# First MoE weight column of batch 0 multiplied inside the last attention units

## The chip, the core and the metric

The kernel runs on one NeuronCore of a Trainium2 chip. The core has five engines with queues of their own: PE (TensorE, matmuls), DVE (VectorE), ACT (ScalarE), POOL (GpSimd, which also issues DMAs here) and SP (SyncE, which here only issues DMAs). Each queue runs its instructions strictly in the order in which they were written, and semaphores hold an instruction until what it reads, or the buffer it overwrites, is ready. The metric is the time of one execution on the device in microseconds (us); lower is better.

## The reference, cut to what matters

```
scores = scale * q @ k.T ; mix the 12 heads by w_pre
attn   = exp(scores - max) / (sum + 1e-9) ; mix the 12 heads by w_post
x      = attn @ v, written as tokens x (12 heads * 64) = 1792 x 768
out    = ((x @ w_a) * (x @ w_b)) @ w_out          # 768 -> 1536 -> 768
```

There are 4 batches of 448 tokens. The second half is called MoE below, after the names in the code.

## The kernel before, in words

**Attention.** The queries of a batch are cut into units of 20 tokens, 23 units per batch, 92 in all, numbered 0 to 91. One loop (lines 695 to 729) writes the program: in its step s it writes unit s's parts for all engines. On PE these are the head mixing `mp` (L308), one score product for a later chunk of queries (`pst`, L244; up to step 82 only), one slice of attn @ v (`xp`, L387) and the second head mixing `pp` (L351) of unit s-1. DVE takes the row maximum `nm` (L318), a copy of the score product in two units of three, and, once ACT has summed the exponentials, three small operations (L331 to L334). ACT computes the exponentials (L321) and copies `pp` out of PSUM (L366). POOL issues the DMAs (L288) that gather unit s+4's scores into `sb`. SP loads q, k and v, stores x to DRAM (`xd`), and once per unit writes one number of `nm` (`paced`, L202), which keeps its queue at the pace of the units. The last steps, 92 and 93, and the code behind the loop finish the last slices of `xp`.

**MoE.** Every product is made of three fp32r matmuls of 448 columns per 128-row block: high half of the weights times both halves of x, and low half of the weights times the high half of x. A column is 128 of the 1536 hidden features. For one column and one batch, `run_a` (into `pa`) and `run_b` (into `pb`) take 18 matmuls each (6 blocks of 3); ACT copies `pa` to `sa`, DVE multiplies `pb` by it into `hf`. So that weights and x are ready in halves, two preparations exist:

- The weights come as 64-bit floats. `to_f32` makes 32-bit floats of one side (w_a or w_b) of a column with six DVE operations and one POOL addition (L502 to L508), then ACT and POOL split them into `wh` and `wl` (L538, L539). `r` (`cvr`) has one buffer, `m` (`cvm`) three.
- x of batch b is loaded from `xd` by six DMAs (`load_x`, L465), and split per block by one ACT copy (L471) and one DVE subtraction (L472).

`order` is the list of the conversions: entry 0 is w_a of column 0, entry 1 is w_b of column 0, entry 2 is w_a of column 1. `plan_moe` puts the first of this work into the attention loop by tables: `todo_at[s]` runs at the start of step s, `at_end[s]` at its end. `s0` is 83. Before the change the weights of entries 0 and 1 are loaded in three DMAs of 256 KB each in units 74 to 76 and 78 to 80; the conversion of entry 0 stands at the ends of steps 78 to 83, that of entry 1 at 84 to 89, and x(0) is loaded in steps 81 to 86 and split in steps 90 to 92. All MoE matmuls stand behind the loop, from `run_a(0, 0)` on.

`plan_loads` distributes q, k and v loads over the steps: each has a first and a last step, and takes the one with the fewest bytes planned so far.

Of the kernel before, what the change touches and what calls it, by code (L numbers as in the profile page):

```python
# [21 lines left out]
def talking_heads_bilinear_kernel(  # L22
# [11 lines left out]
    nc = tc.nc  # L34
# [86 lines left out]
    def ps_t():  # L121
        return ps.tile([128, 2, 512], F32, tag="t", name="pst", bufs=1)[:, 0]
# [3 lines left out]
    def later(fn, n=3):  # L126
        todo_at.setdefault(now[0] + n, []).append(fn)
# [295 lines left out]
    def plan_loads():  # L423
        per_b, row = NC // B, 4 * 128
        wants, busy = [], [0] * (NU + 8)
        for (a, p), u in av_at.items():
            if p % 3 == 2 and u < NU:
                busy[u + 1] += row * 3 * QU * groups[a][2]
        for u in range(V_FIRST, V_FIRST + V_PIECES // 2):
            busy[u] += row * S  # L430
        for c in range(3, NC):
            b, t0, n = chunks[c]
            for j in range(G // QG):
                last = qk_at[c, QG * j] - LEAD
                wants.append((max(last, 0), max(last - 2, 0), row * QG * n, (load_q, c, j)))
            for i in range(G if t0 == 0 else 0):
                n = G * b + i - 10
                first = qk_at[per_b * (n // G) + per_b - 1, n % G] + 1 if n >= 0 else 0
                wants.append((qk_at[c, i] - LEAD, first, row * S, (load_k, b, i)))
        for b in range(1, B):  # L440
            first = max(av_at[per_b * (b - 2) + per_b - 1, H // 2 - 1] + 1 if b > 1 else 0, V_FIRST + V_PIECES // 2)
            for i in range(V_PIECES):
                wants.append((av_at[per_b * b, i // 2] - V_LEAD, first, row * S // 2, (load_v, b, i)))
        for last, first, n, it in sorted(wants, key=lambda w: w[0]):
            u = min(range(min(first, last), last + 1), key=lambda u: (busy[u], -u))
            busy[u] += n
            after.setdefault(u, []).insert(0, it)
# [46 lines left out]
    def to_f32(u):  # L494
        t = raws.pop(u)
        lo, hi = t[:, :, 0], t[:, :, 1]
        m = mc.tile([128, CW], I32, tag="m", name="cvm", bufs=3)
        r = mc.tile([128, CW], I32, tag="r", name="cvr", bufs=1)
        mf = m.bitcast(F32)
        ts, stt = nc.vector.tensor_scalar, nc.vector.scalar_tensor_tensor  # L500
        return m.rearrange("p (k f) -> p k f", k=KD), [
            lambda: ts(m, hi, 0x7FFFFFFF, None, op0=ALU.bitwise_and),  # L502
            lambda: ts(r, lo, 28, 1, op0=ALU.logical_shift_right, op1=ALU.bitwise_and),
            lambda: ts(mf, mf, F64_TOP, 2.0**-112, op0=ALU.min, op1=ALU.mult),
            lambda: ts(m, m, 3, None, op0=ALU.logical_shift_left),
            lambda: stt(m, hi, -(1 << 31), m, op0=ALU.bitwise_and, op1=ALU.bitwise_or),
            lambda: stt(m, lo, 29, m, op0=ALU.logical_shift_right, op1=ALU.bitwise_or),  # L507
            lambda: nc.gpsimd.tensor_tensor(m, m, r, op=ALU.add),  # L508
        ]

    def conv_f(u):
        kind, f, e = u
# [42 lines left out]
    def run_a(f, b):  # L555
        hh, ll = wt["f", f]
        x = xt[b]
        pa = ps.tile([128, 512], F32, tag="m", name="pa", bufs=3)[:, :S]
        mm3(pa, hh, ll, x[:, 0], x[:, 1], KD)
# [4 lines left out]
    def run_b(f, b):  # L564
        hh, ll = wt["f", f]
        x = xt[b]
        pb = (ps_t() if f == b == 0 else ps.tile([128, 512], F32, tag=f"p{b % 2}", name="pb", bufs=1))[:, :S]
        mm3(pb, hh, ll, x[:, 0], x[:, 1], KD, KD)
# [49 lines left out]
    def plan_moe():  # L618
        o, fin = {}, {}

        def at(n, *fns):
            at_end.setdefault(n, []).extend(fns)

        def load(n, fns):
            for i, fn in enumerate(fns):
                todo_at.setdefault(n + i, []).append(fn)

        def op(u, j):
            def run():
# [8 lines left out]
        todo_at.setdefault(RAW_AT[0], []).append(lambda: load(RAW_AT[0] + 1, load_raw(order[0], 3)))
        todo_at.setdefault(RAW_AT[1], []).append(lambda: load(RAW_AT[1] + 1, load_raw(order[1], 3)))
        s0 = last_prep + 1  # L640
        for j in range(KD):
            at(s0 - 5 + j, op(0, j))
            at(s0 + 1 + j, op(1, j))
            todo_at.setdefault(s0 - 2 + j, []).append(lambda j=j: load_x(0, (j,)))
# [12 lines left out]
    with tc.manual_schedule():
# [37 lines left out]
        for s in range(NU + 2):  # L695
            now[0] = s
            if s == last_prep + 1:
                open_moe()
            while nxt_g <= min(s + AH, NU - 1) and ready.get(units[nxt_g][0], -1) < s:
                gather(nxt_g)  # L700
                nxt_g += 1
            if 0 <= s - V_FIRST < V_PIECES // 2:
                for p in range(2):
                    load_v(0, 2 * (s - V_FIRST) + p)
            for fn in todo_at.pop(s, ()):
                fn()
            if s < NU:
                premix(s)
            if 2 <= s <= NU:
                evac_p(s - 2)  # L710
            if s < NU:
                for k_ in blocks_of(s):
                    smax(k_)
            for it in items.get(s, ()):
                if it[0] is qk:
                    it += (it[2] % OWN if s not in late else 1,)
                it[0](*it[1:])
            if s < NU:
                norm(s)
            if 0 <= s - 1 < NU:  # L720
                postmix(s - 1)
            for it in late.get(s, ()):
                qk(*it[1:], 0)
            for it in after.get(s, ()):
                it[0](*it[1:])
            for fn in at_end.pop(s, ()):
                fn()
            if s == NU:
                evac_p(NU - 1)
        for p in range(6):  # L730
            av(NA - 1, p)
        for t in sorted(todo_at):
# [130 lines left out]
```

## Time and profile before

| | us |
|---|---|
| three runs | 899.97, 918.04, 918.10 |
| median of the runs | 918.04 |
| the profiled execution, its own time | 903.93 |
| its span, first to last instruction | 902.2 |
| PE busy in the span | 868.3 (96%) |
| DVE busy | 518.8 (57%) |
| POOL busy | 442.5 (49%) |
| ACT busy | 377.5 (42%) |

The profile is of one execution. PE's matmuls overlap one another, so PE can be counted as busy and still not run at its densest: a matmul of 448 columns is counted with 0.36 us, while the next one starts 0.20 us later. A bracket at the end of a row of the timeline gives the idle time of the engine ahead of that row and what ended it; "issue" there means that the engine waited for nothing that the profile shows. Times in the rows are from the start of the span.

### The profile page before, as it was taken

How to read it: one execution, taken by the hardware profiler on the slowest of the kernel's cores; microseconds unless marked ns; L12 is line 12 of the kernel's file. 1: busy time of each engine (PE TensorE's matmuls, PEld its weight loads, DVE VectorE, ACT ScalarE, POOL GpSimd, SP SyncE). 2: the span in 40 equal slices, each digit the busy share in tenths (PEclk: the TensorE clock that was granted, in tenths of full speed). 3: DMA queues.
4: the chain of work that ended last, by engine and by line, in shares of the span. 5: the costliest groups of instructions: out<-in, count | busy, mean ns of one | idle time of the engine just before them, and what ended most of it. 6: DMA issues, size and time to landing. Idle time of an engine off the chain costs nothing.

```text
span 902.2 us, 27078 instructions
## 1 busy us (share of the span) xinstructions
PE 868.3 (96%) x11440; PEld 703.2 (78%) x11440; DVE 518.8 (57%) x907; ACT 377.5 (42%) x848; POOL 442.5 (49%) x547
## 2 busy tenths in 40 slices
PE   8888999999999897899999999999999999999998
PEld 3455666565666554699999999999999989999997
DVE  5666777677777675577656665557554545151500
ACT  5666777667677665531111111111111244343531
POOL 4586777677766754124333432233232245455552
PEclk9999999999999999999999999999999999999999
DMA  6797676767666965734533433334332664646441
GB/s 161 175 212 182 177 196 191 172 181 188 181 162 180 213 179 126 228 135 136 171 118 124 153 124 136 118 119 136 118 126 87 240 245 149 258 136 258 140 147 61
DMA packets 81850, 147.45 MB, mean 163 GB/s; under 512 B 41758, under 2 KB 61322, under 8 KB 80706
## 3 DMA queue, kind: packets, MB, share of 16 engines
q1 hardware_dynamic: 53602, 108.05, 37.4%
q0 software_dynamic: 28128, 37.68, 16.5%
q8 instruction: 90, 1.47, 0.7%
q14 instruction: 30, 0.25, 0.1%
HBM read 80.23 MB, written 26.74 MB: 119 GB/s over the span
## 4 chain that ended last, share of the span: by engine, by line
PE 76%; POOL 8%; issue 6%; DMA 5%; DVE 2%; ACT 1%; SPq 1%; POOLq 0%; ACTq 0%; DVEq 0%
POOL sb L288 6%; PE pa L549 6%; PE pa L550 6%; PE pa L551 6%; PE po L550 6%; PE po L551 6%; PE po L549 6%; PE pb L550 6%; PE pb L549 6%; PE pb L551 6%; PE xp L387 6%; PE pp L351 5%; PE mp L308 4%; PE pst L244 4%; DMA sb<-s 2%
## 5 line engine op out<-in xcount | busy, mean ns | idle before, releaser
L288 POOL DMA_DIRECT2D sb<-s x350 | 202.6, 589 | 91.1 <-PE mp L308 49.3
L508 POOL TENSOR_TENSOR cvm<-cvm,cvr 128x768 int32<-128x768 int32 x36 | 66.4, 1844 | 196.9 <-DVE cvm L507 196.9
L318 DVE TENSOR_REDUCE nm<-mp 124x1 f32<-124x448 f32 x180 | 104.6, 619 | 67.5 <-PE mp L308 66.4
L539 POOL TENSOR_TENSOR wl<-v,wh 128x768 fp32r<-128x768 f32 x48 | 93.4, 1965 | 100.7 <-ACT wh L538 100.7
L321 ACT ACTIVATE a<-mp,nm 124x448 f32<-124x448 f32 x180 | 112.8, 631 | 57.5 <-DVE nm L318 57.4
L387 PEld LDWEIGHTS xp<-pt,v 120*64 120x64 f32 x1536 | 76.5, 140 | 67.2 <-issue 45.2
L561 ACT COPY sa<-pa 128x448 f32<-128x448 f32 x48 | 25.8, 537 | 227.6 <-PE pa L551 227.6
L351 PE MATMUL pp<-kr,a 60*56 60x60 f32 x5760 | 104.6, 216 | 13.4 <-issue 12.8
L351 PEld LDWEIGHTS pp<-kr,a 60*56 60x56 f32 x5760 | 90.1, 127 | 31.4 <-issue 20.6
L366 ACT COPY pt<-pp 120x480 f32<-120x480 f32 x176 | 91.2, 574 | 50.8 <-PE pp L351 50.7
L308 PE MATMUL mp<-sb,wp 60*64 60x448 f32 x720 | 100.9, 545 | 6.4 <-ACT a L321 3.0
L571 DVE TENSOR_TENSOR hf<-pb,sa 128x448 f32<-128x448 f32 x47 | 29.4, 625 | 132.6 <-PE pb L551 118.8
L550 PE MATMUL po<-hl,wh 128*128 128x448 f32 x288 | 104.5, 363 | 0.7 <-DVE hl L586 0.7
L549 PE MATMUL pa<-xhl,wh 128*128 128x448 f32 x288 | 104.5, 363 | 0.0
L550 PE MATMUL pa<-xhl,wh 128*128 128x448 f32 x288 | 104.4, 362 | 0.0
L551 PE MATMUL pa<-xhl,wl 128*128 128x448 f32 x288 | 104.4, 362 | 0.0
L551 PE MATMUL po<-hh,wl 128*128 128x448 f32 x288 | 104.4, 362 | 0.0
L549 PE MATMUL po<-hh,wh 128*128 128x448 f32 x288 | 104.4, 362 | 0.0
L551 PE MATMUL pb<-xhl,wl 128*128 128x448 f32 x282 | 102.2, 362 | 0.0
L549 PE MATMUL pb<-xhl,wh 128*128 128x448 f32 x282 | 102.2, 362 | 0.0
L550 PE MATMUL pb<-xhl,wh 128*128 128x448 f32 x282 | 102.2, 362 | 0.0
L586 DVE TENSOR_TENSOR hl<-hl,hh 128x448 fp32r<-128x448 f32 x48 | 57.5, 1253 | 75.9 <-ACT hh L585 75.9
(75 smaller groups left out, 1377.7 us busy)
## 6 DMA issues: line engine op xcount, KB each, us to landing
sb<-s POOLq DMA_DIRECT2D x346, 105.0 KB, 4.6
v<-wod SPq DMA_DIRECT2D x24, 768.0 KB
v<-in_w_ab_dram SPq DMA_DIRECT2D x22, 768.0 KB
hd<-hf SPq DMA_DIRECT2D x48, 224.0 KB
v<-in_w_out_dram SPq DMA_DIRECT2D x12, 768.0 KB
k<-in_k_dram SPq DMA_DIRECT2D x24, 224.0 KB
v<-in_v_dram SPq DMA_DIRECT2D x48, 112.0 KB
xhl<-xd SPq DMA_DIRECT2D x24, 224.0 KB
```

The source lines that it names most:

```text
L288: (nc.sync if u <= AH and i % 2 else nc.gpsimd).dma_start(out=sbt[u][i % 2][r:r + m * H], in_=rows)
L308: nc.tensor.matmul(mt[u, i // 2][col:col + M], lhsT=wp[r:r + m, :M], rhs=tiles[i % 2][r:r + m])
L318: nc.vector.tensor_reduce(nm[:m], mp[:m], axis=AXX, op=ALU.max, negate=True)
L321: nc.scalar.activation(a[:m], mp[:m], ACTF.Exp, bias=nm[:m], scale=1.0, accum_out=rss[u][:m, j:j + 1])
L351: nc.tensor.matmul(pp_t[i][64 * e:64 * e + C, H * r:H * r + H, j, :m], lhsT=a[rows, keys:keys + C], rhs=kr[rows, j, :, :m],)
L366: nc.scalar.copy(to[:C2, :, o + QB * i:o + QB * i + QB], pp_t[i][:C2].rearrange("p x j t -> p x (j t)"))
L387: nc.tensor.matmul(xp[64 * e:64 * e + 64, p % 3, :n], lhsT=vt[b % 2][g][:C2, h % G, r], rhs=ptt[a][:C2, r, h, :n], start=(r == 0), stop=(r ...
L508: lambda: nc.gpsimd.tensor_tensor(m, m, r, op=ALU.add),
L539: nc.gpsimd.tensor_tensor(ll[:, sl], raw, hh.bitcast(F32)[:, sl], op=ALU.subtract)
L549: nc.tensor.matmul(o, lhsT=hh[:, k0 + kk], rhs=mh[:, kk], start=(kk == 0), stop=False)
L550: nc.tensor.matmul(o, lhsT=hh[:, k0 + kk], rhs=ml[:, kk], start=False, stop=False)
L551: nc.tensor.matmul(o, lhsT=ll[:, k0 + kk], rhs=mh[:, kk], start=False, stop=(kk == n - 1))
```

## The change

The conversion of entry 0 (w_a of column 0) leaves `to_f32` and is done in two halves of three blocks each, in buffers of its own: six DMAs of 128 KB at the ends of steps 50 to 52 and 62 to 64, the six DVE operations and the POOL addition on half the width in steps 56 to 62 and 68 to 74, ACT's and POOL's split in steps 64 and 76, into a new tile `wa`. Entry 1 takes the places that entry 0 had (steps 78 to 86), with its raw weights loaded in steps 75 to 77. x(0) is loaded in steps 78 to 83 and split one block per step in 82 to 87. The 36 matmuls of column 0 and batch 0 are written in pieces: one block of the `a` side (3 matmuls) at the end of each of steps 84 to 89, two blocks of the `b` side (6 matmuls) at the ends of 90 and 91, and the last two blocks behind the loop. Behind the loop, the splitting of x(1) (`split_all(1)`) now stands ahead of the last 48 + 48 matmuls of `xp` and of DVE's two copies of them; before, it stood behind. The loads of entries 2 and later and of x(1) to x(3) keep their steps.

```diff
-    RAW_AT = (73, 77)
+    RAW_AT = 74
+    FIRST = 50
+    FIRST_LEAD = 6
+    FIRST_HALF = 12
...
+        for i in range(KD):
+            u = FIRST + FIRST_HALF * (i // KH) + i % KH
+            wants.append((u, u, 2 * row * 128, ((lambda i=i: mo["load_first"](i)),)))
...
+    def product(f, b, e, o, k0, k1):
+        hh, ll = wt["a"] if f == e == 0 else wt["f", f]
+        x, off = xt[b], 0 if f == e == 0 else e * KD
+        for k in range(k0, k1):
+            first, last = k == 0, k == KD - 1
+            nc.tensor.matmul(o, lhsT=hh[:, off + k], rhs=x[:, 0, k], start=first, stop=False)
+            nc.tensor.matmul(o, lhsT=hh[:, off + k], rhs=x[:, 1, k], start=False, stop=False)
+            nc.tensor.matmul(o, lhsT=ll[:, off + k], rhs=x[:, 0, k], start=False, stop=last)
...
+    def part_of(e, k0, k1):
+        if not early:
+            early["t"] = ps.tile([128, 2, 512], F32, tag="t", name="pst", bufs=1)
+        o = early["t"][:, e, :S]
+        product(0, 0, e, o, k0, k1)
+        if k1 == KD:
+            (take_b if e else take_a)(0, 0, o)
...
+        def first_split(h):
+            raw = piece(h, "m").bitcast(F32).rearrange("p (k f) -> p k f", k=KH)
+            hh, ll = (wa[:, i, KH * h:KH * h + KH] for i in range(2))
+            nc.scalar.copy(hh, raw)
+            nc.gpsimd.tensor_tensor(ll, raw, hh.bitcast(F32), op=ALU.subtract)
...
+        for h in range(2):
+            n = FIRST + FIRST_LEAD + FIRST_HALF * h
+            for j in range(7):
+                at(n + j, lambda h=h, j=j: first_op(h, j))
+            at(n + 8, lambda h=h: first_split(h))
+        todo(RAW_AT, lambda: load(RAW_AT + 1, load_raw(order[1], 3)))
         for j in range(KD):
-            at(s0 - 5 + j, op(0, j))
-            at(s0 + 1 + j, op(1, j))
-            todo_at.setdefault(s0 - 2 + j, []).append(lambda j=j: load_x(0, (j,)))
-        at(s0 + 4, op(0, 6))
-        at(s0 + 5, lambda: fin[0]())
-        at(s0 + 7, op(1, 6), *xs(0))
-        at(s0 + 8, *xs(1), lambda: fin[1]())
-        at(s0 + 9, *(fn for m in range(2, KD) for fn in xs(m)))
+            at(s0 - 5 + j, op(1, j))
+            todo(s0 - 5 + j, lambda j=j: load_x(0, (j,)))
+            at(s0 - 1 + j, *xs(j))
+        at(s0 + 1, op(1, 6))
+        at(s0 + 3, lambda: fin[1]())
+        for k in range(KD):
+            at(s0 + 1 + k, lambda k=k: part_of(0, k, k + 1))
+        at(s0 + 7, lambda: part_of(1, 0, 2))
+        at(s0 + 8, lambda: part_of(1, 2, 4))
...
+        part_of(1, 4, KD)
+        for fn in split_all(1):
+            fn()
         for p in range(6):
             av(NA - 1, p)
...
-        stage(996)
-        run(split_all(1))
-        run_a(0, 0)
+        stage(997)
         ops2, fin2 = conv(order[2])
         run(ops2)
-        run_b(0, 0)
-        stage(997)
```

How the order of the instructions moves, at the two places that the prediction speaks of.

DVE from the end of step 83 on (`cvm` and `cvr` are the buffers of a conversion, `xhl` is x split in halves, `nm` the row maximum that begins a unit, `rs`, `rc` and `kr` the three small operations that end it). Before:

```order
L507 SCALAR_TENSOR_TENSOR cvm<-v_108,cvm 128x768
L318 TENSOR_REDUCE nm<-mp 124x1 x2
L396 COPY xs<-xp 128x360
L331 TENSOR_SCALAR rs<-rs 124x2
L332 RECIPROCAL rc<-rs 124x2
L334 TENSOR_TENSOR kr<-kf,rc 124x120
L502 TENSOR_SCALAR cvm<-v_109 128x768
L318 TENSOR_REDUCE nm<-mp 124x1 x2
L331 TENSOR_SCALAR rs<-rs 124x2
L332 RECIPROCAL rc<-rs 124x2
L334 TENSOR_TENSOR kr<-kf,rc 124x120
L503 TENSOR_SCALAR cvr<-v_109 128x768
```

After:

```order
L479 TENSOR_TENSOR xhl<-xhl 128x448
L510 SCALAR_TENSOR_TENSOR cvm<-v_109,cvm 128x768
L322 TENSOR_REDUCE nm<-mp 124x1 x2
L400 COPY xs<-xp 128x360
L335 TENSOR_SCALAR rs<-rs 124x2
L336 RECIPROCAL rc<-rs 124x2
L338 TENSOR_TENSOR kr<-kf,rc 124x120
L479 TENSOR_TENSOR xhl<-xhl 128x448
L322 TENSOR_REDUCE nm<-mp 124x1 x2
L335 TENSOR_SCALAR rs<-rs 124x2
```

The conversion at the end of step 83 stays, with a subtraction for x(0) ahead of it. The operations of the second conversion behind it, among them the one at the end of step 85 that writes `cvr`, are gone; steps 84 to 87 have one subtraction each in their place.

DVE and PE from the end of the loop on (`hf` is the product of the two sides of a column, `xs` the copy of `xp`). DVE before, then after:

```order
L396 COPY xs<-xp 128x360
L396 COPY xs<-xp 128x3x88 x2
L472 TENSOR_TENSOR xhl<-xhl 128x448 x6
L502 TENSOR_SCALAR cvm<-v_108 128x768
L503 TENSOR_SCALAR cvr<-v_108 128x768
```

```order
L400 COPY xs<-xp 128x360
L582 TENSOR_TENSOR hf<-pst,sa 128x448
L479 TENSOR_TENSOR xhl<-xhl 128x448 x6
L400 COPY xs<-xp 128x3x88 x2
L505 TENSOR_SCALAR cvm<-v_108 128x768
```

The six subtractions of x(1) moved from behind the two last copies `xs` to ahead of them, and `hf` of column 0, which stood behind the conversion that begins with L502, went ahead of both. PE after, at the same place:

```order
L391 MATMUL xp<-pt,v_111 64x120 x8
L570 MATMUL pst<-xhl,wh 128x448
L571 MATMUL pst<-xhl,wh 128x448
L572 MATMUL pst<-xhl,wl 128x448
L391 MATMUL xp<-pt,v_110 64x88 x24
L391 MATMUL xp<-pt,v_111 64x88 x24
L570 MATMUL pa<-xhl,wa 128x448
```

The three rows on `pst` stand twice there. Before, `pa` of batch 0 followed the last `xp`; now `pa` of batch 1 does.

## Rows read from the trace of the kernel before

**Rows 1.** Windows: start:end, length, busy us of PE, PEld, DVE, ACT, POOL, PEclk, DMA share, GB/s

```profile
250.00:300.00 50.00, 48.51 (x1320) 30.71 (x1316) 34.79 (x81) 34.86 (x86) 34.96 (x63) 1.00 0.69 177
349.60:353.00 3.40, 3.37 (x26) 1.82 (x26) 2.24 (x6) 2.33 (x7) 0.00 (x0) 0.54 0.00 0
372.90:376.60 3.70, 3.49 (x48) 3.23 (x48) 0.17 (x1) 1.46 (x4) 0.00 (x0) 0.55 0.67 250
```

**Rows 2.** Timeline of DVE: start, length, line, operation, count, idle before and its end

```profile
150.12 1.16 DVE L318 TENSOR_REDUCE nm<-mp 124x1 f32<-124x448 f32 x2 [0.75 <-PE mp L308]
157.07 0.62 DVE L318 TENSOR_REDUCE nm<-mp 124x1 f32<-124x448 f32 x1 [0.68 <-PE mp L308]
...
300.95 1.14 DVE L318 TENSOR_REDUCE nm<-mp 124x1 f32<-124x448 f32 x2
326.52 1.16 DVE L318 TENSOR_REDUCE nm<-mp 124x1 f32<-124x448 f32 x2 [1.23 <-PE mp L308]
```

**Rows 3.** Waits of PE, 332 to 380: total us, times, longest us

```profile
PE mp L308 <- ACT a L321: 3.0, 1, 3.0
PE xp L387 <- DVE xs L396: 2.5, 2, 2.0
```

**Rows 4.** Timeline of DVE, units 83 to 91

```profile
333.65 1.15 DVE L318 TENSOR_REDUCE nm<-mp 124x1 f32<-124x448 f32 x2
336.34 0.95 DVE L507 SCALAR_TENSOR_TENSOR cvm<-v,cvm 128x768 int32<-128x768 int32 x1
337.21 1.15 DVE L318 TENSOR_REDUCE nm<-mp 124x1 f32<-124x448 f32 x2
340.89 1.16 DVE L318 TENSOR_REDUCE nm<-mp 124x1 f32<-124x448 f32 x2 [0.44 <-PE mp L308]
347.66 0.56 DVE L503 TENSOR_SCALAR cvr<-v 128x768 int32<-128x768 int32 x1 [3.99 <-POOL cvm L508]
348.14 1.15 DVE L318 TENSOR_REDUCE nm<-mp 124x1 f32<-124x448 f32 x2
358.62 1.16 DVE L318 TENSOR_REDUCE nm<-mp 124x1 f32<-124x448 f32 x2
365.69 0.62 DVE L318 TENSOR_REDUCE nm<-mp 100x1 f32<-100x448 f32 x1
```

**Rows 5.** Timeline of POOL

```profile
345.21 0.59 POOL L288 DMA_DIRECT2D sb<-s  x1 [0.41 <-issue]
345.81 1.82 POOL L508 TENSOR_TENSOR cvm<-cvm,cvr 128x768 int32<-128x768 int32 x1
386.85 1.83 POOL L508 TENSOR_TENSOR cvm<-cvm,cvr 128x768 int32<-128x768 int32 x1 [16.63 <-DVE cvm L507]
```

**Rows 6.** Timeline of PE

```profile
339.43 0.58 PE L351 MATMUL pp<-kr,a 60*56 60x60 f32 x27 [1.61 <-issue]
360.37 1.00 PE L308 MATMUL mp<-sb,wp 60*64 60x448 f32 x8
363.16 0.93 PE L308 MATMUL mp<-sb,wp 60*64 60x448 f32 x4
372.89 3.50 PE L387 MATMUL xp<-pt,v 120*64 120x88 f32 x48 [1.99 <-DVE xs L396]
376.92 2.04 PE L387 MATMUL xp<-pt,v 120*64 120x88 f32 x48 [0.53 <-DVE xs L396]
378.89 0.47 PE L549 MATMUL pa<-xhl,wh 128*128 128x448 f32 x1
386.19 0.36 PE L549 MATMUL pa<-xhl,wh 128*128 128x448 f32 x1
```

**Rows 7.** Timeline of DVE, end of attention

```profile
376.43 0.43 DVE L396 COPY xs<-xp 128x264 f32<-128x264 f32 x1 [3.68 <-PE xp L387]
379.48 3.30 DVE L472 TENSOR_TENSOR xhl<-xhl 128x448 fp32r<-128x448 f32 x6
387.22 4.63 DVE L472 TENSOR_TENSOR xhl<-xhl 128x448 fp32r<-128x448 f32 x6
```

More of the change, by code (lines that the diff above doesn't have):

```diff
@@ L50, in talking_heads_bilinear_kernel @@
     CW = KD * 128
+    KH = KD // 2
     AH = 4
@@ L492, in new_w, with bits @@
         return wt[key]
[L494 to L498, printed above, removed]
+    def bits(lo, hi, m, r):
         mf = m.bitcast(F32)
         ts, stt = nc.vector.tensor_scalar, nc.vector.scalar_tensor_tensor
-        return m.rearrange("p (k f) -> p k f", k=KD), [
+        return [
             lambda: ts(m, hi, 0x7FFFFFFF, None, op0=ALU.bitwise_and),
@@ L509, in to_f32 @@
         ]
+    def to_f32(u):
+        t = raws.pop(u)
+        n = mo["m"] = mo.get("m", -1) + 1
+        m = (mo["w"] if n % 3 == 2 else mc).tile([128, CW], I32, tag="m", name="cvm", bufs=1 if n % 3 == 2 else 2)
+        r = mc.tile([128, CW], I32, tag="r", name="cvr", bufs=1)
+        return m.rearrange("p (k f) -> p k f", k=KD), bits(t[:, :, 0], t[:, :, 1], m, r)
     def conv_f(u):
@@ L553, in talking_heads_bilinear_kernel, with take_a @@
     sas = {}
[L555 to L559, printed above, removed]
+    def product(f, b, e, o, k0, k1):
[6 more added lines that the diff above has]
+            nc.tensor.matmul(o, lhsT=ll[:, off + k], rhs=x[:, 0, k], start=False, stop=last)
+    def take_a(f, b, pa):
         sa = sb_p.tile([128, S], F32, tag="sb0", name="sa")
@@ L562, in run_a, with take_b @@
         sas[f, b] = sa
[L564 to L568, printed above, removed]
+    def take_b(f, b, pb):
         sa = sas.pop((f, b))
@@ L572, in run_b, with run_a @@
         later(lambda: nc.sync.dma_start(out=hd[b][:, f], in_=hf), 1)
+    def run_a(f, b):
+        pa = ps.tile([128, 512], F32, tag="m", name="pa", bufs=3)[:, :S]
+        product(f, b, 0, pa, 0, KD)
+        take_a(f, b, pa)
+    def run_b(f, b):
+        pb = ps.tile([128, 512], F32, tag=f"p{b % 2}", name="pb", bufs=1)[:, :S]
+        product(f, b, 1, pb, 0, KD)
+        take_b(f, b, pb)
+    early = {}
+    def part_of(e, k0, k1):
[5 more added lines that the diff above has]
+            (take_b if e else take_a)(0, 0, o)
     ht = {}
@@ L633, in op @@
             return run
+        s0 = last_prep + 1
         def xs(m):
             return [lambda: split_x(0, m)[0](), lambda: split_x(0, m)[1]()]
[L638 to L644 removed]
@@ L645, in plan_moe, with todo, open_first @@
-        at(s0 + 4, op(0, 6))
-        at(s0 + 5, lambda: fin[0]())
-        at(s0 + 7, op(1, 6), *xs(0))
-        at(s0 + 8, *xs(1), lambda: fin[1]())
-        at(s0 + 9, *(fn for m in range(2, KD) for fn in xs(m)))
+        def todo(n, fn):
+            todo_at.setdefault(n, []).append(fn)
+        wa = mc.tile([128, 2, KD, 128], F32R, tag="wa", name="wa")
+        first = {}
+        mo["n"] = 0
+        def open_first():
+            first["m"], first["raw"] = (mc.tile([128, CW], I32, tag="m", name="cvm", bufs=2) for _ in range(2))
+            first["r"] = mc.tile([128, CW], I32, tag="r", name="cvr", bufs=1)
@@ new lines, in load_first, with piece, first_op @@
+        def load_first(k):
+            if not k:
+                open_first()
+            to = first["raw"].rearrange("p (k f) -> p k f", k=KH)[:, k % KH]
+            nc.sync.dma_start(out=to, in_=w_ab[0, 0].bitcast(I32)[:, k])
+        def piece(h, x):
+            return first[x][:, KH * 128 * h:KH * 128 * (h + 1)]
+        def first_op(h, j):
+            t = first["raw"].rearrange("p (c t) -> p c t", t=2)
+            bits(t[:, :, 0], t[:, :, 1], piece(h, "m"), piece(h, "r"))[j]()
+        def first_split(h):
[3 more added lines that the diff above has]
+            nc.gpsimd.tensor_tensor(ll, raw, hh.bitcast(F32), op=ALU.subtract)
```

4 lines of the change are left out of this document (3 added, 1 removed).

## The prediction

> **What bounds the kernel now.** I read the page first: PE is busy for 96% of the span, so only what shortens PE's path can shorten the kernel. The windows then say that this holds in the attention loop too: 48.5 us of 50 busy at a granted clock of 1.00 [rows 1]. The timeline of DVE gives the pace: two units from 150.12 to 157.07, 3.48 us each, each beginning after a wait for PE [rows 2]. So up to unit 82, where the score products end, the loop goes at PE's pace, and DVE has some 0.7 us to spare per unit.
>
> The place that the change touches is different. The waits of PE from 332 to 380 show one of 3.0 us for ACT and two of 2.5 us in all for DVE's copies of `xp` [rows 3]. The first starts on POOL. DVE's operation L503 writes `cvr` and waits 3.99 us until POOL has finished the addition L508 of the first conversion, which has the same buffer [rows 4]; L508 stands behind the last gathers in POOL's queue and runs only at 345.81 [rows 5]. DVE's next row maximum comes 7.25 us after the one before it (340.89 to 348.14), and ACT and PE with it. Behind each of the two long waits the granted clock is near its lower level (1.2 GHz of 2.4): 0.54 from 349.6 and 0.55 from 372.9, against 1.00 [rows 1]. The two groups of 48 matmuls at the end show the price: 3.50 us the first, 2.04 us the second [rows 6].
>
> In units 83 to 91 PE has less to do: from 360.37 to 363.16, 2.79 us a unit [rows 6]. The row maxima still come 3.5 us apart, (365.69 - 348.14) / 5 [rows 4]. There DVE's own sequence sets the pace: from a row maximum to the end of the three small operations 2.69 us (333.65 to 336.34), then 0.55 to 0.95 us of conversion [rows 4]. PE has some 0.7 us per unit to give away, and this is what the change uses.
>
> **The change, part by part.** I follow one path: from unit 82 to the first matmul of `run_a(0, 1)`, at 386.19 now [rows 6]. All that lies behind is a stream of matmuls and moves with it as one.
>
> *The column leaves the stream.* Its 36 matmuls take from 378.89 to 386.19 [rows 6]: **-7.3 us**. They come back in other places, priced below at 0.2 us each, the step in the stream (7.3 / 36).
>
> *The wait for POOL goes.* Only one full-width conversion is left ahead of the end of the loop, so nothing on DVE waits there for L508. The 7.25 us become 3.48: **-3.8 us**. The lower clock behind it costs little now, since DVE keeps its pace there (3.49 us a unit from 348.14 to 358.62 [rows 4]), so nothing is counted for it.
>
> *Steps 82 and 83* get one subtraction of x(0) each beside a conversion of 0.95 us. Six of them take 3.30 us [rows 7], 0.55 each; DVE has nothing left to hide it: **+1.1 us**. ACT's copy for it is done while DVE runs the small operations.
>
> *Steps 84 to 91.* In 84 to 87 a subtraction replaces a conversion of about the same length: 0. In 84 to 89 PE gets 3 matmuls per unit, 2.79 + 0.6 = 3.4 us, about DVE's pace: they are hidden, at a gain of 0.3 us in unit 84 (3.68 us now, 337.21 to 340.89 [rows 4]) and 0.3 in 88 and 89, where DVE loses its conversions. If the cover is gone, the 18 cost 3.6 us. Step 90 gets 6 matmuls: 2.79 + 1.2 = 4.0, against 3.5: +0.5. Sum: **-0.1 us**, so that the row maximum of unit 91 comes at 365.69 - 3.8 + 1.1 - 0.1 = 362.9.
>
> *From there to the stream* it is 13.2 us now (365.69 to 378.89), with a wait of 2.0 us and the slow group in it. After: PE has `xp` 1.0, `pp` 0.9, 6 matmuls 1.2, `xp` 1.0, `pp` 0.8, `xp` 1.0, 6 matmuls 1.2, in all 7.1 us, then 2.04 for the first 48. But the last 48 need DVE's copy of the first, and in DVE's queue it now stands behind `hf` (0.6) and the six subtractions of x(1) (3.3), which start only when the last pieces are multiplied: 7.1 + 0.6 + 3.3 + 0.4 for the copy [rows 7] = 11.4. PE is ready at 9.1 and waits 2.3 us. That lies between waits of 2.0 and 3.0 us, which were followed by the lower clock, and above the 1.61 us at 339.43 [rows 6], which was not. I take the price again, 1.5 us. 11.4 + 2.0 + 1.5 = 14.9: **+1.7 us**; without the lower clock +0.2.
>
> *Units 50 to 76.* 12 half-width DVE operations (0.3 to 0.5 us, half of L503 and L507 [rows 4]), within the 0.7 us to spare; 2 ACT copies; 4 POOL operations of 0.9 us, half of L508. Value **+0.5 us**; best case 0.
>
> A row speaks against this. Six subtractions took 3.30 us at 379.48 and 4.63 us at 387.22 [rows 7], where POOL's addition ran from 386.85 to 388.68 [rows 5]: 1.3 us more. If each of the four new POOL operations holds up DVE for its whole length, it is 3.7 us. The Trainium skill, page "SBUF — State Buffer", section "SBUF: two separate sides", has a rule that agrees with this row: VectorE and GpSimd share one pair of ports, as a lock held for a whole instruction. By that rule the term would be up to 3.7 us instead of 0.5. I stay near the low end, since DVE waits 0.7 us per unit for PE there [rows 2].
>
> *The loads.* No byte is added. Half of the raw weights, 6 times 128 KB, move from units 74 to 76 to units 50 to 52 and 62 to 64, and x(0) moves 3 units ahead. Near the raw loads, the six units from 300.95 to 326.52 took 25.6 us against 6 x 3.48 = 20.9 [rows 2]: 4.7 us lost. Less load there could give back up to 3 us, and the new places could lose as much: 0, with ±3. On SP the loads stand between the numbers that pace the queue, and nothing waits for them for 4 units.
>
> *Behind the path.* After its last copy DVE has six operations of the next conversion, about 4 us, before it splits x(2), and x(2) is needed 7.2 us after the stream begins: hidden with 2 to 3 us to spare.
>
> Sum: 7.3 + 3.8 - 1.1 + 0.1 - 1.7 - 0.5 = 7.9, say **8 us less**. The profiled execution, 903.93 us (a span of 902.2 and 1.7 around it), becomes 896. The median of the three runs, 918.04, lies 14.1 us above it, and the lowest run 4 us below; the profile of one execution does not show why. The median is what is asked for, so the forecast is 918.04 - 8 = **910 us**.
>
> **The rivals.**
>
> *More is won.* The lower clock does not come back (1.5 us), and the lighter loads near units 74 to 80 give 3 us: 12.5 us less, 905.5. For it: the loss there stands in rows. Against it: the wait at the end is longer than the one now. Chance 0.17.
>
> *Less is won.* POOL's operations hold up DVE in units 56 to 76 (3.2 us more than in the sum), or the pieces in units 84 to 89 lie on PE's path (3.6 us). Either alone leaves 4.5 us: 913.5. The first is also what the page's rule on the ports gives. For it: the 1.3 us at 387.22. Chance 0.20.
>
> *Slower.* POOL's queue runs dry of gathers. Each new POOL operation waits for DVE or ACT of its unit, and the gathers behind it wait too. If one is late by more than its lead, PE stops; a stop like that at 346 costs 3.8 us, and 1.5 more for the lower clock, since PE sets the pace there. From the second on the gain is gone; with the five that are possible (four, and the addition in step 84) it ends at 910 + 26.5 = 936.5. Against it: the last gather was issued at 345.21 [rows 5] and its unit began on PE at 363.16 [rows 6], 18 us later, while a wait of one unit is 3.5 us. Chance 0.04.
>
> *It does not do what it says:* x(0) or the weights are late and the pieces wait in PE's queue, so that the column costs there what it cost before: 918. Against it: both are due two units ahead. Chance 0.03.
>
> **How the numbers follow.** The forecast, a gain of 5.5 to 11 us, has 0.56. Its own range on the median is 907 to 913. The three runs lie 18 us apart, though, and a median of three may fall on the lower level: 900 - 13 = 887 at best. Upwards I stop at a gain of 3 on the upper one: 915. So 887 to 915 holds about 0.85 of it all. Two per cent, 18 us, is about what a measurement of this kernel can tell from no change, as its own runs are that far apart. No case above wins 18 us by its mechanism; the new median would have to fall on the lower level while the old one stays on the upper. I give that 0.26. Slower by over 2% needs the third rival: 0.04. The rest, 0.70, is within 2%.
>
> **What would show it.** In the changed kernel's profile: no wait of DVE for POOL's addition in units 84 to 87, and row maxima about 3.4 us apart from unit 84 to 89; three matmuls on `pst` per unit there, without PE waiting for them; DVE's copies of `xp` behind six subtractions, and a wait of PE of about 2.3 us ahead of the last 48 matmuls, with the clock near 0.5 behind it; the first matmul of `run_a(0, 1)` 8 us earlier than 386.19. I am wrong if units 56 to 76 take longer than 3.5 us each, if DVE waits for ACT's copies at 82 to 87, or if the stream of matmuls behind waits for x(2).

## The result, and the profile after

Twenty runs of the changed kernel have a median of 899.73 us (893.39 to 913.3), twenty of the kernel before 911.67 us (899.97 to 923.86). The ratio is 0.9902 [0.9876, 0.9928]; it leaves runs at a disturbed, slower level out of both sides. Of 911.67 us it is 8.9 us, by the interval 6.6 to 11.3. So the kernel became faster by about 1%, under the 2% that was called distinguishable. The forecast gain was 8 us, the forecast time 910 us. That time is 10.3 us too high. Of this, 6.4 us come from its starting point: the median of the first three runs, 918.04, lies that far above the median of twenty. The other 3.9 us are the distance of the two medians, 11.9 us, from the 8 us of the forecast.

The profiled execution of the changed kernel took 901.0 us with a span of 899.3. Of its page, first the busy shares, then the chain of work that ended last, by engine; the third line is the same chain in the kernel before:

```profile
PE 870.1 (97%) x11440; PEld 701.3 (78%) x11440; DVE 520.6 (58%) x913; ACT 376.4 (42%) x849; POOL 441.6 (49%) x549
PE 91%; issue 2%; DVE 2%; SPq 2%; DMA 1%; ACT 1%; POOL 0%; ACTq 0%; DVEq 0%; POOLq 0%
PE 76%; POOL 8%; issue 6%; DMA 5%; DVE 2%; ACT 1%; SPq 1%; POOLq 0%; ACTq 0%; DVEq 0%
```

PE is 97% busy, and 91% of the chain is its own. The smaller share of POOL is not to be read as the change's doing: most of the 8% before are gathers (L288), and in a second profile of the kernel before POOL has 2%. The timeline of DVE (start, length, line, operation, idle time before it) answers to [rows 4] and [rows 7]; the row maxima are now L322, the subtractions L479:

```profile
334.76 1.16 DVE L322 TENSOR_REDUCE nm<-mp 124x1 f32<-124x448 f32 x2 [1.31 <-PE mp L312]
337.73 0.62 DVE L479 TENSOR_TENSOR xhl<-xhl 128x448 fp32r<-128x448 f32 x1 [0.19 <-issue]
338.27 0.95 DVE L509 SCALAR_TENSOR_TENSOR cvm<-v,cvm 128x768 int32<-128x768 int32 x1
339.14 1.15 DVE L322 TENSOR_REDUCE nm<-mp 124x1 f32<-124x448 f32 x2
343.24 1.14 DVE L322 TENSOR_REDUCE nm<-mp 124x1 f32<-124x448 f32 x2
346.46 1.15 DVE L322 TENSOR_REDUCE nm<-mp 124x1 f32<-124x448 f32 x2
349.68 1.15 DVE L322 TENSOR_REDUCE nm<-mp 124x1 f32<-124x448 f32 x2
...
360.68 1.16 DVE L322 TENSOR_REDUCE nm<-mp 124x1 f32<-124x448 f32 x2 [0.91 <-PE mp L312]
364.37 1.16 DVE L322 TENSOR_REDUCE nm<-mp 124x1 f32<-124x448 f32 x2 [0.91 <-PE mp L312]
368.60 0.62 DVE L322 TENSOR_REDUCE nm<-mp 100x1 f32<-100x448 f32 x1 [1.46 <-PE mp L312]
...
376.38 3.29 DVE L479 TENSOR_TENSOR xhl<-xhl 128x448 fp32r<-128x448 f32 x6
379.59 0.42 DVE L400 COPY xs<-xp 128x264 f32<-128x264 f32 x1
386.50 6.61 DVE L479 TENSOR_TENSOR xhl<-xhl 128x448 fp32r<-128x448 f32 x6
```

The reader sees units 82 and 83 at 4.38 and 4.10 us, with a subtraction beside a conversion at 337.73; then units 84 and 85 at 3.22 us, where unit 85 took 7.25 before; and at the end of the loop, behind 360.68, waits of 0.9 to 1.5 us for PE. DVE sets the pace up to 85, PE from 87 on. The timeline of PE shows why, and answers to [rows 6]:

```profile
362.47 0.47 PE L570 MATMUL pst<-xhl,wa 128*128 128x448 f32 x1
363.28 0.98 PE L312 MATMUL mp<-sb,wp 60*64 60x448 f32 x8
366.16 0.47 PE L570 MATMUL pst<-xhl,wh 128*128 128x448 f32 x1
367.56 0.96 PE L312 MATMUL mp<-sb,wp 60*64 60x448 f32 x4
...
375.74 2.04 PE L391 MATMUL xp<-pt,v 120*64 120x88 f32 x48
380.07 2.04 PE L391 MATMUL xp<-pt,v 120*64 120x88 f32 x48 [2.30 <-DVE xs L400]
382.05 0.47 PE L570 MATMUL pa<-xhl,wa 128*128 128x448 f32 x1
392.63 0.47 PE L571 MATMUL pa<-xhl,wa 128*128 128x448 f32 x1 [0.52 <-DVE xhl L479]
894.91 0.36 PE L561 MATMUL po<-hh,wl 128*128 128x448 f32 x1
```

A piece of 3 matmuls takes 0.81 us (362.47 to 363.28), one of 6 takes 1.40 (366.16 to 367.56). The stream begins at 382.05 against 386.19 before, although this execution came to unit 82 later (334.76 against 330.10). The whole stretch from the row maximum of unit 82 to the last matmul, which holds the column, the wait and the end of attention, fell from 568.06 us (330.10 to 898.16) to 560.15 (334.76 to 894.91): 7.9 us less. Its two ends in the kernel before:

```profile
330.10 1.15 DVE L318 TENSOR_REDUCE nm<-mp 124x1 f32<-124x448 f32 x2
898.16 0.36 PE L551 MATMUL po<-hh,wl 128*128 128x448 f32 x1
```

This **path length** is what I compare below. Units 0 to 82, in which an execution differs from the next by some us, are not in it. It is one profile for each kernel; a second of the changed kernel (after_again) has 1.2 us more.

### The profile page after: what moved, and what is told of

Its sections match the earlier page's. It is cut to its first block, busy times and chain, and to the rows that moved or that the text cites. A ratio compares the mean times of both kernels' runs of the same rounds, so it can differ in the third digit from the quotient of the medians.

```text
span 899.3 us, 27085 instructions
## 1 busy us (share of the span) xinstructions
PE 870.1 (97%) x11440; PEld 701.3 (78%) x11440; DVE 520.6 (58%) x913; ACT 376.4 (42%) x849; POOL 441.6 (49%) x549
## 4 chain that ended last, share of the span: by engine, by line
PE 91%; issue 2%; DVE 2%; SPq 2%; DMA 1%; ACT 1%; POOL 0%; ACTq 0%; DVEq 0%; POOLq 0%
PE pp L355 9%; PE xp L391 9%; PE mp L312 8%; PE pst L248 8%; PE po L560 6%; PE po L561 6%; PE pa L571 6%; PE po L559 6%; PE pa L572 6%; PE pa L570 6%; PE pb L571 6%; PE pb L570 6%; PE pb L572 6%; DMA sb<-s 1%; DVE xhl L479 1%
## 5 line engine op out<-in xcount | busy, mean ns | idle before, releaser
L511 POOL TENSOR_TENSOR cvm<-cvm,cvr 128x768 int32<-128x768 int32 (+1 forms) x37 | 66.9, 1807 | 211.1 <-DVE cvm L510 211.1
L322 DVE TENSOR_REDUCE nm<-mp 124x1 f32<-124x448 f32 x180 | 104.5, 618 | 70.3 <-PE mp L312 69.9
L355 PE MATMUL pp<-kr,a 60*56 60x60 f32 (+1 forms) x5760 | 102.5, 216 | 12.6 <-issue 12.5
L355 PEld LDWEIGHTS pp<-kr,a 60*56 60x56 f32 (+1 forms) x5760 | 88.9, 127 | 29.8 <-issue 19.2
L248 PE MATMUL pst<-k,q 64*64 64x448 f32 (+1 forms) x728 | 96.0, 553 | 2.6 <-ACT s L275 1.4
L391 PE MATMUL xp<-pt,v 120*64 120x120 f32 (+1 forms) x1536 | 94.8, 267 | 2.9 <-DVE xs L400 2.3
L570 PE MATMUL pa<-xhl,wh 128*128 128x448 f32 x264 | 95.7, 362 | 0.0
```

What stands on the lines that cost most here:

```text
L248: nc.tensor.matmul(out[64 * e:64 * e + cols.stop - cols.start], lhsT=qt[c, i // QG][rows, i % QG, cols], rhs=kt[b, i][rows],)
L355: nc.tensor.matmul(pp_t[i][64 * e:64 * e + C, H * r:H * r + H, j, :m], lhsT=a[rows, keys:keys + C], rhs=kr[rows, j, :, :m],)
L391: nc.tensor.matmul(xp[64 * e:64 * e + 64, p % 3, :n], lhsT=vt[b % 2][g][:C2, h % G, r], rhs=ptt[a][:C2, r, h, :n], start=(r == 0), stop=(r ...
L570: nc.tensor.matmul(o, lhsT=hh[:, off + k], rhs=x[:, 0, k], start=first, stop=False)
```

## The experiments

The theory: the gain is the column taken out of the stream plus the wait for POOL, and some of it is given back in units 82 to 91 and at the last copies. The rivals: the wait alone is worth it; the placing of the column does not matter; the work in units 50 to 76 costs several us; the lower clock behind the wait at 380 costs it.

**Only the wait (b_two_r, on the kernel before).**

```diff
-        r = mc.tile([128, CW], I32, tag="r", name="cvr", bufs=1)
+        r = mc.tile([128, CW], I32, tag="r", name="cvr", bufs=2)
```

> The kernel before with one edit: cvr gets two buffers, so that DVE's operation of the second conversion in unit 85 need not wait for POOL's addition of the first. Theory: the row maxima of units 85 and 86 come 3.5 us apart instead of 7.25, the lower clock behind the wait is gone, and the kernel is 3.8 us faster than before (ratio 0.996). Rival: the units behind make the wait up, since PE has time to spare there; then the last row maximum comes at the same distance from that of unit 82 as before (35.6 us) and the time is that of before.

Measured: 910.26 us, ratio 0.997 [0.9937, 1.0003], 2.7 us less. The DVE timeline of this kernel (its own line numbers, those of before):

```profile
344.21 1.15 DVE L318 TENSOR_REDUCE nm<-mp 124x1 f32<-124x448 f32 x2
346.94 0.55 DVE L503 TENSOR_SCALAR cvr<-v 128x768 int32<-128x768 int32 x1
347.41 1.15 DVE L318 TENSOR_REDUCE nm<-mp 124x1 f32<-124x448 f32 x2
350.10 2.69 DVE L504 TENSOR_SCALAR cvm<-cvm 128x768 f32<-128x768 f32 x1
352.72 1.14 DVE L318 TENSOR_REDUCE nm<-mp 124x1 f32<-124x448 f32 x2
```

and of POOL, and a window (start:end, length, busy us of PE, PEld, DVE, ACT, POOL, granted clock, DMA share, GB/s):

```profile
350.54 1.83 POOL L508 TENSOR_TENSOR cvm<-cvm,cvr 128x768 int32<-128x768 int32 x1
368.50:378.70 10.20, 8.77 (x123) 7.87 (x123) 3.36 (x7) 6.85 (x15) 1.81 (x1) 0.50 0.75 236
```

The wait of L503 is gone (7.25 us become 3.20). But the addition now runs while DVE goes on, and DVE's next operation, L504, takes 2.69 us beside it, where the median of its 36 in this kernel is 0.55. Unit 86 takes 5.31 us instead of 3.32. At the end the clock is at its lower level for 10.2 us, and from unit 91 to the stream it is 14.95 us against 13.19. The path length is 566.77: of 4 us won, 1.3 are left. Neither forecast came as it was put: the wait went, and the units behind did not make it up (from unit 82 to 91 it is 32.56 us against 35.60), but unit 86 gave 2.0 us back and the end 1.8, while the other units were 1.0 shorter together. The wait for POOL had kept a collision with POOL away. That the lower clock at the end comes from this edit is not shown. The change has the same addition in this place, in its timeline of POOL:

```profile
343.40 1.82 POOL L511 TENSOR_TENSOR cvm<-cvm,cvr 128x768 int32<-128x768 int32 x1 [1.52 <-DVE cvm L510]
```

Beside it stands the row maximum of 343.24, which reads PSUM, with its usual 1.14 us, and no L507 (the L504 of before) follows, so units 84 and 85 keep their 3.22 us.

**The column in one piece behind the loop (a_column_behind, on the kernel after).**

```diff
-            at(s0 + 1 + k, lambda k=k: part_of(0, k, k + 1))
-        at(s0 + 7, lambda: part_of(1, 0, 2))
-        at(s0 + 8, lambda: part_of(1, 2, 4))
...
-        part_of(1, 4, KD)
+        part_of(0, 0, KD)
+        part_of(1, 0, KD)
```

> The changed kernel with all 36 matmuls of the first column behind the loop, nothing else moved. Theory as the prediction put it: 18 matmuls in units 84 to 89 are hidden, so this costs 3.6 us or more against the changed kernel and wins 4 to 5 us on before. Rival: the pieces lie on PE's path in the units (87 to 89 take 3.69 us in the changed kernel, 2.8 without them), and what was won is the wait for POOL and the earlier x(0); then this is only about 2 us slower than the changed kernel, and 6 to 7 faster than before.

Measured: 904.0 us, ratio 0.9938 [0.9905, 0.9971], 3.3 us above the change's 0.9902; the intervals overlap, but the path length says the same, 563.79 against 560.15, 3.6 us more. Its DVE timeline at units 89 to 91:

```profile
355.79 1.16 DVE L322 TENSOR_REDUCE nm<-mp 124x1 f32<-124x448 f32 x2 [0.35 <-PE mp L312]
358.51 1.16 DVE L322 TENSOR_REDUCE nm<-mp 124x1 f32<-124x448 f32 x2
361.26 0.62 DVE L322 TENSOR_REDUCE nm<-mp 100x1 f32<-100x448 f32 x1
```

Without pieces and conversions units 89 and 90 take 2.7 us instead of 3.7 and 4.2. From unit 82 to 91 it is 3.7 us shorter, and from 91 to the stream 7.0 us longer. In the changed kernel 24 of the 36 matmuls are multiplied ahead of the row maximum of unit 91 and 12 behind it, so 24 moved, 4.8 us at the step of 0.2. Of these 4.8 us the pieces hide only 1.1: they pay 3.7 in the loop, nothing in units 84 and 85 and all of it in 86 to 90. There a unit takes 3.6 to 4.2 us with a piece and 2.7 to 3.4 without. The other 2.2 of the 7.0 us lie in what the column meets in one piece: a gap of PE at 363.55, a wait for ACT's copy `sa`, and the lower clock from 380.7, in which the last 48 matmuls take 2.46 us instead of 2.04. Of its timeline of PE:

```profile
366.56 0.48 PE L570 MATMUL pst<-xhl,wa 128*128 128x448 f32 x1
371.08 0.47 PE L570 MATMUL pst<-xhl,wh 128*128 128x448 f32 x1 [0.62 <-ACT sa L576]
374.88 2.04 PE L391 MATMUL xp<-pt,v 120*64 120x88 f32 x48
379.28 2.46 PE L391 MATMUL xp<-pt,v 120*64 120x88 f32 x48 [2.37 <-DVE xs L400]
```

So the theory's 3.6 us came, but only in part for its reason: 1.1 us of it is matmuls that the loop hides.

**The last copies ahead of the split of x(1) (a_copy_first), and x(2) split ahead of the next conversion as well (a_copy_conv).**

```diff
         part_of(1, 4, KD)
+        for p in range(3):
+            av(NA - 1, p)
         for fn in split_all(1):
             fn()
-        for p in range(6):
+        for p in range(3, 6):
             av(NA - 1, p)
...
+        run(split_all(2))          # a_copy_conv only
         ops2, fin2 = conv(order[2])
         run(ops2)
-        run(split_all(2))          # a_copy_conv only
```

> The changed kernel with the splitting of x(1) written behind the first 48 of the last matmuls on xp and their copy, instead of ahead of them. Theory: PE's wait of 2.3 us ahead of the last 48 matmuls goes, but DVE now waits for the first copy and reaches x(2) later, so that the wait turns up on PE in batch 2 of the column: 0 to 1.5 us slower than the changed kernel. Rival: the stream begins 2.3 us earlier and stays so: 2.3 us faster than the changed kernel.

> As the run with the copy first, and DVE's conversion of the next weights (entry 2) written behind the splitting of x(2) instead of ahead of it. Theory: neither the wait of 2.3 us ahead of the last matmuls on xp nor the 0.7 us for x(2) is left: 3 us faster than the changed kernel, 11 to 12 faster than before. Rival: a wait turns up elsewhere, at x(3) or at the second column, whose weights come 3 us later: as the changed kernel.

Measured: a_copy_first 901.62 us, ratio 0.9899 [0.9866, 0.9932], path 561.19. Of its waits of PE from 360 to 400 (total us, times, longest):

```profile
PE pa L571 <- DVE xhl L479: 2.4, 2, 1.2
PE xp L391 <- DVE xs L400: 0.5, 1, 0.5
```

The wait of 2.3 us at the copy became 0.5, and two waits of the stream for the split x took its place: the wait moved, and nothing was won. a_copy_conv: 896.61 us, ratio 0.9871 [0.9832, 0.9911], path 557.86. Its timeline of PE and DVE:

```profile
374.42 2.04 PE L391 MATMUL xp<-pt,v 120*64 120x88 f32 x48 [0.54 <-DVE xs L400]
376.38 0.48 PE L570 MATMUL pa<-xhl,wa 128*128 128x448 f32 x1
377.96 3.30 DVE L479 TENSOR_TENSOR xhl<-xhl 128x448 fp32r<-128x448 f32 x6
```

Now x(2)'s subtractions run alone, 3.30 us, and are ready in time. The path is 2.3 us shorter than the change's, where 3 were forecast.

**The work of units 50 to 76 (a_no_first, a_loads_only), beside unchanged copies of both kernels (after_again, before_again).**

```diff
-        for i in range(KD):                                        # a_no_first only
-            u = FIRST + FIRST_HALF * (i // KH) + i % KH            # a_no_first only
-            wants.append((u, u, 2 * row * 128, ((lambda i=i: mo["load_first"](i)),)))
...
-            n = FIRST + FIRST_LEAD + FIRST_HALF * h
-            for j in range(7):
-                at(n + j, lambda h=h, j=j: first_op(h, j))
-            at(n + 8, lambda h=h: first_split(h))
+            nc.vector.memset(wa[:, h].bitcast(F32), 0.01)
```

> The changed kernel without the loads and the conversion of w_a of column 0 in units 50 to 76; its tile is filled with a constant ahead of the loop, so that side of the column is not the reference's. It prices all that the change put into units 50 to 76. Theory: 0.5 us for the work and about 0 for the loads, so at most 1 us faster than the changed kernel, and units 50 to 82 as long as in the kernel before (120 us in its profile, 124 in the one run of it with two cvr buffers). Rival: that work costs what the profile of the changed kernel shows there beside the first profile of before, 3.6 us.

> The same, but the six loads of 128 KB stay and only their conversion is left out. Theory: as without loads, within what can be measured; units 50 to 82 within 1 us of it. Rival (instruction fetches of PE collide with the loads): all of the extra time of the changed kernel in units 50 to 64 is here too, and this is as slow as the changed kernel.

> The changed kernel once more, for a second profile and as a control in this call. From unit 82 to the end as in its first profile, 560 us within 1, with PE's wait of 2.3 us ahead of the last matmuls on xp; units 0 to 82 may differ by several us, as PE's gaps behind instruction fetches fall elsewhere. The wait of 2.3 us is followed by the lower clock or not, as its place in time happens to be.

> The kernel before once more, for a second profile: unit 82 to the end 568 us within 1 if the two waits and the lower clock behind them belong to the program; units 50 to 82 between 120 and 124 us.

Measured: a_no_first 901.39 us, 0.9891 [0.9851, 0.9932]; a_loads_only 900.55, 0.9891 [0.9853, 0.9929]; after_again 902.48, 0.9902 [0.9869, 0.9935]; one run of before_again, 915.4. By the times the work costs 0.0011, 1 us, which these intervals cannot tell from nothing.

The profiles give the stretches. From the row maximum of unit 56 to that of unit 65, where the first half of the work stands, it took 36.7 us on average in the eight profiles that have the work (35.9 to 37.8) and 34.7 in the five without it (32.9 to 36.1). The highest of the five is a_loads_only, so the ranges overlap, and the 2.0 us between the averages are not shown to be the work's. Units 74 to 82, where the raw loads were thinned, took 30.8 us in the ten profiles with fewer loads there (29.6 to 31.7) and 32.6 in the three with before's loads (31.9 to 33.3). Cost and gain are of one size. Units 50 to 82 as a whole scatter too much to decide anything: 122.4 us in a_no_first, 126.1 in a_loads_only, which was forecast within 1 us of it, and 121.2 to 126.6 in the eight with the work.

The paths: after_again has 561.31, 1.2 more than the first profile and just outside its forecast of 560 within 1; a_no_first has 560.92 and a_loads_only 560.13, so this work does not touch the path. before_again has 574.28 and not 568 within 1. Both waits and the lower clock behind them came again there; 5.5 of the 6.2 us more lie in the output matmuls at the end (last section), with nothing in the program that differs.

after_again shows the step that I had forecast and not found. A window of it, 1.4 us after the same wait of 2.3 us, and then the first profile as far behind its wait:

```profile
382.20:385.40 3.20, 3.20 (x23) 2.79 (x19) 2.00 (x5) 0.00 (x0) 0.00 (x0) 0.50 0.20 46
```

```profile
381.50:384.70 3.20, 3.20 (x31) 2.94 (x26) 2.47 (x6) 0.00 (x0) 0.00 (x0) 1.00 0.30 67
```

Behind the same wait the granted clock falls to 0.50, its lower level of 1.2 GHz, in one execution, and stays at 1.00 in the other.

**x(0) two units later (a_later_x), the split of x(2) alone (a_conv_only), and a_copy_conv once more.**

```diff
-            at(s0 - 1 + j, *xs(j))
+            at(s0 + 1 + j, *xs(j))                             # a_later_x, on a_copy_conv
...
-            at(s0 + 1 + k, lambda k=k: part_of(0, k, k + 1))
+            at(s0 + 2 + k, lambda k=k: part_of(0, k, k + 1))   # part_of(1, 0, 2) at s0 + 8, the rest behind
```

> The run with the copy first and the conversion behind x(2), and besides x(0) split in steps 84 to 89 instead of 82 to 87, the pieces of the a side in 85 to 90, 6 matmuls of the b side in 91 and 12 behind the loop. Theory: units 82 and 83 take 3.56 us again instead of 4.38 and 4.09 (-1.3 us), unit 90 3.7 instead of 4.2, and 6 matmuls more lie behind the loop (+1.2): 0.7 us less from unit 82 to the end than in that run, about 557 us. Rival: the subtractions only move the loss to units 88 and 89: no gain.

> The changed kernel with DVE's conversion of entry 2 behind the splitting of x(2), nothing else. Theory: the six subtractions of x(2) no longer run beside POOL's addition and subtraction and take 3.3 us instead of 6.6; PE does not wait for them; its wait of 2.3 us ahead of the last matmuls on xp stays: 0.7 us less than the changed kernel where that one has the wait for x(2), and nothing that the times can tell. Rival: the subtractions are slow for another reason and take over 5 us again.

> The run with the copy first and the conversion behind x(2) once more, as the control for the run with x(0) later: ratio to the kernel before 0.987 within 0.004, unit 82 to the end 558 us within 1.

Measured: a_later_x 900.94 us, 0.984 [0.979, 0.9891], path 558.24; a_copy_conv_again 901.7, 0.9905 [0.9863, 0.9946], path 558.14; a_conv_only 898.9, 0.9891 [0.9838, 0.9944], path 561.04. The path of a_later_x equals that of a_copy_conv, so the theory of 0.7 us less missed: units 82 and 83 win 1.3 us and unit 90 0.6, but units 84 to 86 lose 1.1, at 3.50, 3.57 and 4.19 us, and the six matmuls more behind the loop cost 1.2. Its better ratio, from few runs, is therefore not explained by the edit, and with the overlap of the intervals I do not count it. In a_conv_only the subtractions of x(2) run alone again, in 3.3 us as forecast, and the wait for x(2) is gone. But that wait is gone in after_again and a_no_first too, where the lower clock behind the wait of 2.3 us came, as it did here; so what this edit is worth alone is not shown. On the path neither edit alone gains (561.19 and 561.04) and both together gain 2 us, in two profiles. In times that gain is not confirmed: its two ratios, 0.9871 and 0.9905, lie on both sides of the change's 0.9902. No version is shown to beat the change in time.

## Why the prediction was right, point by point

| Step | forecast, us | measured, us |
|---|---|---|
| column leaves the stream | -7.3 | -7.3 |
| wait for POOL (unit 85: 7.25 to 3.22) | -3.8 | -4.0 |
| units 82, 83 | +1.1 | +1.4 |
| units 84, 86 to 90 | -0.1 | +0.9 |
| unit 91 to the stream | +1.7 | +0.2 |
| behind the path | 0 | +0.9 |
| sum on the path | -8.4 | -7.9 |
| units 50 to 76 | +0.5 | +1 by the times, +2 by the profiles, not resolved |
| loads thinned, units 74 to 82 | 0, with ±3 | -1.8 |

The first row is the same reading of the kernel before on both sides, so it tests nothing by itself; what the 36 matmuls cost in their new places is in the rows below it. That the sum comes so near is in part luck: units 82 to 90 without unit 85, and the stream behind, cost 2.2 us more than forecast, and unit 91 to the stream 1.5 us less, because the lower clock did not come.

**The column and the wait** are right in mechanism and size. b_two_r shows that taking the wait away by itself is worth less: it wins 4.0 us at unit 85 and loses 2.0 of them at once to the collision, and 1.3 are left on its path. In the change the conversion that collided is gone as well, and units 85 and 86 have no such loss.

**Units 84 to 91** were mis-sized. I priced a matmul of a piece at 0.2 us, the step inside the stream. Set between the matmuls of attention, 3 cost 0.81 and 6 cost 1.40, some 0.2 us more per piece, and units 87 to 89 take 3.69 us where I had 3.4. That is above DVE's pace, so PE sets it there (the waits of 0.9 us at 360.68 and 364.37). The prediction counted on DVE's pace of 3.5 us as cover; in a_column_behind DVE needs only 2.7 us in units 89 and 90, so there was nothing left to hide behind where its conversions and subtractions had ended. This is a part of the rival "less is won": the pieces lie partly on PE's path. a_column_behind gives its size, 3.7 us paid in the loop for 24 matmuls of 4.8 us.

**From unit 91 to the stream** the wait of 2.30 us came exactly where and as long as the sum of DVE's queue had it. The lower clock that I added, 1.5 us, did not follow in this profile, and did in after_again, a_column_behind, a_no_first and a_conv_only (in a_loads_only it did not). This step was right about the wait and wrong to count the clock as certain. Its price was too high as well: where it came behind this wait, the stretch from unit 91 to the stream took 13.9 to 14.2 us instead of 13.4 (a_column_behind left aside, which has more matmuls there), 0.5 to 0.8 us and not 1.5. On the whole it hardly matters: where the lower clock came, the stream met no wait for x(2) behind it, and the paths of the change and its copy differ by 1.2 us.

**Behind the path** I forecast x(2) hidden with 2 to 3 us to spare, and this step failed. Its six subtractions began at 386.50 and took 6.61 us, twice the 3.29 of the same six at 376.38. PE waited at 392.63, 0.52 us; a_copy_conv, without this wait, needs 0.6 us less from the beginning of the stream to the output matmuls, and the other 0.3 of the 0.9 us are not traced. The timeline of POOL shows what ran beside them (idle time before, and what ended it):

```profile
386.67 2.15 POOL L511 TENSOR_TENSOR cvm<-cvm,cvr 128x768 int32<-128x768 int32 x1 [30.74 <-DVE cvm L510]
389.77 2.33 POOL L549 TENSOR_TENSOR wl<-cvm,wh 128x768 fp32r<-128x768 f32 x1 [0.95 <-ACT wh L548]
```

I had read the same slowing in [rows 7], where six took 4.63 us, and used it only for units 56 to 76; here I took the durations as they are alone. The view of these six by their line gives the shortest, the median and the longest in ns:

```profile
L479 DVE TENSOR_TENSOR xhl<-xhl x6: 611/616/2277, 386.5 to 392.5; 128x448 fp32r<-128x448 f32 x6
```

One by one in the trace, four take 0.61 or 0.62 us and two 2.27 and 2.28. Those two begin at 387.04 and 390.30, while the addition and the subtraction of POOL are running, and end 0.5 us after POOL's operation has ended. In a_copy_conv, where the subtractions stand ahead of the conversion, they take 3.30 us.

**Units 50 to 76**, where I feared this slowing, had little of it. The timeline of the changed kernel at one of the two half-width additions and at the subtraction behind it:

```profile
258.95 1.00 POOL L511 TENSOR_TENSOR cvm<-cvm,cvr 128x384 int32<-128x384 int32 x1 [1.17 <-DVE cvm L510]
259.66 1.16 DVE L322 TENSOR_REDUCE nm<-mp 124x1 f32<-124x448 f32 x2 [0.80 <-PE mp L312]
269.81 0.99 POOL L699 TENSOR_TENSOR wa<-cvm,wa 128x384 fp32r<-128x384 f32 x1 [5.18 <-ACT wa L698]
270.17 0.77 DVE L338 TENSOR_TENSOR kr<-kf,rc 124x120 f32<-124x120 f32 x1
```

DVE's next operation beside the addition is a row maximum, which reads PSUM, and it has its usual 1.16 us. Beside the subtraction `kr` takes 0.77 us instead of 0.28; beside the other addition and the other subtraction (303.89 and 313.48) no operation of DVE is longer than usual. (The conversion there uses the two `cvm` buffers and the one `cvr` of the others; new is only `wa`.) So POOL's operations lengthened DVE's by 0.5 us here, not 3.7; where the 2 us of the profiles come from, if they are real, is open.

**The signs of being wrong.** Two of the three came. The stream waited for x(2), as said. Units 56 to 76 took 3.76 us each, over the 3.5 that I had set; but the kernel before has 3.65 there in its profile, so this sign was set where it could not tell. DVE had no wait for ACT's copies in units 82 to 87.

**The chances.** The forecast case was the one that came. The slower rival, POOL running dry, does not show: PE has no wait for a gather from 235 to 345, where the four new POOL operations and the addition lie, and DVE none for POOL from 332 to 390. The time of 910 us has the error of its base in it, and the range, 887 to 915, held because it was made wide for just that.

What stays open: why the lower clock follows the same wait in one execution and not in another, and whether the work of units 50 to 76 costs nothing, 1 us or 2.

## What to carry to other kernels

Before work is moved into another engine's idle time, price it at what it costs between that engine's other instructions, not at its step in a dense stream, and see which engine then sets the pace. A wait that is taken away lets two engines run together that had run one after the other: look for a collision there, and at what is late next, since three of these edits only moved a wait. Where runs of one kernel lie 18 us apart, compare a path within the trace, and take the base from more than three runs.

## What the hardware showed beyond the forecast

VectorE and GpSimd hold each other up in whole instructions. Of six subtractions two grew from 0.61 to 2.27 and 2.28 us, each until 0.5 us after the GpSimd operation beside it had ended; these two GpSimd operations took 2.15 and 2.33 us, against 1.82 in the units before (343.40 and 353.00). One L504 took 2.69 us and ended 0.4 us after the GpSimd addition beside it. A reduction out of PSUM was not held up (1.14 and 1.16 us). The Trainium skill, page "SBUF — State Buffer", section "SBUF: two separate sides", describes an exclusive lock on a shared port pair, held for a whole instruction by whichever starts first. The traces agree in the lengths, and for the two subtractions in the order: they began 0.37 and 0.53 us after the GpSimd operation. L504 began 0.44 us before the addition, though, and still ended after it; GpSimd was issuing a gather until 350.52, and which of the two held up L504 first is not shown.

Units 0 to 82 differ between executions by up to 6 us. PE's gaps without a releaser ("issue") go with loads of instructions. The larger of the two queues that bring them, in the page's list (packets, MB, share of 16 engines):

```profile
q8 instruction: 90, 1.47, 0.7%
```

Of PE's gaps of 0.5 to 2 us between 45 and 370 us, 14 of 16 (before), 9 of 10 (after), 14 of 14 (after_again) and 9 of 11 (before_again) end 2.0 to 2.9 us after such a packet starts. Some 64 packets fall into these 325 us, so by chance about one gap in five would. No run here took these loads away, so this is a coincidence in time and not a cause shown.

In before_again, some 835 output matmuls in a row stepped at 0.2066 us at a granted clock of 1.00, against 0.200 in the first profile: 5.5 us on its path of 574.28, with nothing in the program that differs. No other profile here has this step; its cause is open.
